# Summing z on VectorE instead of TensorE, with the mask from selects, E built later, six residual buffers and one dm step emptied bank by bank

## The chip, the cores and the metric

The kernel runs on one core of one Trainium2 chip. The metric is the device time of one execution in microseconds (us), and the median of several executions is quoted. A profiled execution lists a span, which is some 2 us shorter than the time of the same execution (819.0 us and 820.84 us for the kernel before).

## The reference

The kernel computes the output and all six gradients of a pre-norm linear-attention block that is followed by a SwiGLU feed-forward network (FFN). S is 2048, D is 640, there are 32 heads of 20 columns, and the FFN is 1728 wide. What matters here is the attention forward and one product of the backward pass that is used as filler.

```python
qkv = layernorm(x) @ wqkv                      # q, k, v: 32 heads of 20
phi = lambda t: where(t > 0, t + 1, exp(t)) + 1e-6
pq, pk = phi(q), phi(k)
kv  = einsum("bhsd,bhse->bhde", pk, v)
z   = einsum("bhsd->bhd", pk)                  # the sum over the 2048 tokens
num = einsum("bhqd,bhde->bhqe", pq, kv)
den = einsum("bhqd,bhd->bhq", pq, z)[..., None] + 1e-6
h   = x + (num / den -> [S, D]) @ wo           # the residual tiles xr are rows of x
out = h + FFN(layernorm(h))                    # and then the gradients of all of it
```

## The kernel before

After the first phase (layer norm, q, k and their phi) come some 93 us that the change touches. TensorE computes Y = xnᵀ·pk (five `ps_y` steps), then the heads' blocks of kv (`ps_kvt`), then W2 (`ps_w2t`, which folds kv and wo together), and last the attention output `ps_a` for 16 row tiles. Steps of an independent product, dm = dout·w_downᵀ (`ps_dm`), are put between them. VectorE divides q by its denominator (`normalise`), and SyncE's transposing loads bring the result into the form that `ps_a` needs (`pqsT`). All matmul results go to one pool of four tiles in PSUM, the memory to which every product here is written. Each tile is `[P, 2, 512]` in fp32, and its two halves are called banks. TensorE reuses a tile when another engine has emptied it: in the trace of this kernel `ps_dm` at 137.19 starts 0.04 us after the end of ScalarE's copy (from 136.34, 0.81 us) for which it waits.

```python
psum = ctx.enter_context(tc.tile_pool(name="psum", bufs=4, space=bass.MemoryType.PSUM))
work = ctx.enter_context(tc.tile_pool(name="work", bufs=5))       # xr, zs, zl and others
# ... the sum z, on TensorE: four groups of tokens, each in 32 rows
        ps = mm("ps_z")
        for ci, (n0, n1) in enumerate(NCH):
            for t in range(ST):
                q = t % 4 * H
                nc.tensor.matmul(ps[q:q + H, ci, :320], lhsT=ones[:, :H], rhs=pk[:, t, n0:n1],
                                 start=(t < 4), stop=(t >= ST - 4))
        zs = [wk("zs"), wk("zl")]                                  # high and low part in bf16
        nc.scalar.copy(out=half(zs[0][:]), in_=row(ps))
        last_zs = nc.vector.tensor_tensor(out=half(zs[1][:]), in0=row(ps), in1=half(zs[0][:]), op=ALU.subtract).ins
# ... a dm step: ten products, one copy by ScalarE
                ps = mm("ps_dm")
                dm_mm(ps, wdT3 if g == 3 else wdT, t, g)
                nc.scalar.copy(out=dst[:, :, :w], in_=ps[:, :, :w])
                if g == 3:
                    nc.scalar.dma_start(out=scr_dm_v[:, t:t + 2, :], in_=dst[:, :, :w])
# ... masks(): E by selects, then mask = Eᵀ E by two matmuls (cut)
# ... normalise(t): q*z, sum per head, + 1e-6, reciprocal, multiply; four row tiles at once (cut)
        for i in range(DT):
            ps = mm("ps_y")
            mm_row(ps, lambda t: xn[:, t, i * P:(i + 1) * P], lambda t, n0, n1: pk[:, t, n0:n1], ST)
            nc.scalar.copy(out=half(Yt[:, i, :]), in_=row(ps))
            if i == 0:
                mm_row(ps_z, lambda k: ones32[:], lambda k, n0, n1: zs[k][:, n0:n1], 2)   # "ps_zb"
                nc.scalar.copy(out=half(zb[:]), in_=row(ps_z))
                masks()
            if 0 < i < 4:
                dm(1)
        dm(1)
        for t in (0, 4):
            normalise(t)
            tr_pqs(t)                      # four transposing loads on SyncE
        for t in range(3):
            load_xr(t)                     # residual tile, on SyncE
        nc.sync.dma_start(out=mat_v(scr_Yt), in_=Yt)
        # ... ps_kvt; dm(1); five ps_w2t with W2's transposes on SyncE, one dm(1) among them
        for t in (8, 12):
            normalise(t)
            tr_pqs(t)
        dm(3)
        for t in range(ST + 2):            # "the loop"
            if t < ST:
                xr = xrs.pop(t)
                ps = mm("ps_a")
                mm_row(ps, lambda i: pqsT[:, i, t * P:(t + 1) * P], lambda i, n0, n1: W2[:, i, n0:n1], DT)
                nc.vector.tensor_tensor(out=half(xr[:]), in0=row(ps), in1=half(xr[:]), op=ALU.add)
                # ... statistics of xr
                dm(1)
            if t > 0:
                load_xr(t + 2)
            u = t - 2
            # ...
            nc.scalar.dma_start(out=scr_h1_v[:, u, :], in_=h1[:])      # h1 is xr of tile u
            # ... hn (VectorE), hnT (a transposing load on SyncE)
```

Note for later what stands in ScalarE's instruction queue in the loop. It issues the stores of `h1` and of the last `dm` group, and between these stores stand its copies that empty the `ps_dm` buffers.

## Time and profile before

| | kernel before |
|---|---|
| time, median of 3 (range) | 821.44 us (821.32 to 822.36) |
| span of the profiled execution, clock | 819.0 us, 1.000 |
| TensorE busy | 812.0 us |
| VectorE / ScalarE / GpSimd busy | 442.4 / 291.0 / 188.2 us |
| first `ps_z` to first `pg` of the FFN, "the stretch" | 55.72 to 149.12 = 93.40 us |
| from the first `pg` to the end | 669.90 us |

The page and TensorE's timeline are read in the prediction below.

### The profile page before, as it was taken

How to read it: one execution, taken by the hardware profiler on the slowest of the kernel's cores; microseconds unless marked ns; L12 is line 12 of the kernel's file. 1: busy time of each engine (PE TensorE's matmuls, PEld its weight loads, DVE VectorE, ACT ScalarE, POOL GpSimd, SP SyncE). 2: the span in 40 equal slices, each digit the busy share in tenths (PEclk: the TensorE clock that was granted, in tenths of full speed). 3: DMA queues.
4: the chain of work that ended last, by engine and by line, in shares of the span. 5: the costliest groups of instructions: out<-in, count | busy, mean ns of one | idle time of the engine just before them, and what ended most of it. 6: DMA issues, size and time to landing. Idle time of an engine off the chain costs nothing.

```text
span 819.0 us, 14057 instructions
## 1 busy us (share of the span) xinstructions
PE 812.0 (99%) x5540; PEld 521.7 (64%) x5540; DVE 442.4 (54%) x874; ACT 291.0 (36%) x412; POOL 188.2 (23%) x345
## 2 busy tenths in 40 slices
PE   8999999999999999999999999999999999999998
PEld 6776656555555555555566677777777777777675
DVE  6878676891077018810660147787793366631212
ACT  6982422770084126500741122322322133322010
POOL 3330022322412312221125301211220111112330
PEclk9999999999999999999999999999999999999999
DMA  9994589999759997894498757977498999999962
GB/s 301 195 356 86 140 175 280 244 226 214 198 123 206 208 207 178 183 249 115 98 233 185 258 123 217 219 206 181 110 224 178 172 174 165 176 204 259 227 177 75
DMA packets 278321, 158.61 MB, mean 194 GB/s; under 512 B 235052, under 2 KB 264877, under 8 KB 278256
## 3 DMA queue, kind: packets, MB, share of 16 engines
q1 hardware_dynamic: 251696, 82.12, 53.1%
q0 software_dynamic: 17744, 64.45, 26.6%
q10 hardware_dynamic: 8816, 11.16, 4.3%
q8 instruction: 43, 0.70, 0.4%
q14 instruction: 22, 0.18, 0.1%
HBM read 47.68 MB, written 53.66 MB: 124 GB/s over the span
## 4 chain that ended last, share of the span: by engine, by line
PE 92%; DVE 4%; ACT 2%; DMA 1%; issue 1%; POOL 0%; DVEq 0%; ACTq 0%
PE ps_dw L627 21%; PE ps_dhn L109 14%; PE ps_dxn L871 8%; PE ps_o L932 7%; PE pu L563 7%; PE pg L558 7%; PE ps_dwqk L109 5%; PE ps_dm L385 5%; PE ps_y L109 3%; PE ps_dp L109 3%; PE ps_dk L109 3%; PE ps_gt L678 3%; PE ps_a L109 3%; PE pdm L385 2%; DVE st L134 1%; ACT phi_e L307 1%
## 5 line engine op out<-in xcount | busy, mean ns | idle before, releaser
L109 PE MATMUL ps_dhn<-wgT,cols 128*128 128x320 bf16 x864 | 119.5, 299 | 0.0
L627 PE MATMUL ps_dw<-dd,hn 128*128 128x448 bf16 (+1 forms) x640 | 118.8, 346 | 0.0
L109 PEld LDWEIGHTS <-cols 128*128 128x128 bf16 x864 | 84.5, 98 | 32.9
L627 PEld LDWEIGHTS <-hn 128*128 128x128 bf16 x640 | 62.6, 98 | 54.2
L629 DVE CAST dwev<-ps_dw 128x896 bf16<-128x896 f32 (+3 forms) x12 | 10.9, 908 | 123.5 <-PE ps_dw L627 123.5
L629 ACT CAST dwev<-ps_dw 128x896 bf16<-128x896 f32 (+1 forms) x20 | 17.6, 878 | 157.9 <-PE ps_dw L627 146.7
L592 POOL DMA_DIRECT2D scr_dT<-stg x64 | 34.8, 543 | 168.7 <-DMA stg<-dd 163.2
L147 DVE CUSTOM_DVE_ANT_0 lb_a<-lb_dy,hn 128x640 bf16<-128x640 bf16 x32 | 26.4, 826 | 75.3 <-ACT lb_dy L145 75.3
L558 PE MATMUL pg<-wgu,hnT 128*128 128x448 bf16 (+1 forms) x320 | 63.6, 346 | 0.0
L563 PE MATMUL pu<-wgu,hnT 128*128 128x448 bf16 (+1 forms) x320 | 63.6, 346 | 0.0
L932 PE MATMUL ps_o<-wd,mT 128*128 128x320 bf16 (+3 forms) x462 | 61.3, 295 | 0.0
L627 PE MATMUL ps_dw<-m_s,dh 128*128 128x448 bf16 (+1 forms) x320 | 60.4, 346 | 0.0
L871 PEld LDWEIGHTS <-ring 128*128 128x128 bf16 x480 | 47.0, 98 | 18.2
L932 PEld LDWEIGHTS <-mT 128*128 128x128 bf16 (+1 forms) x462 | 41.8, 97 | 17.6 <-issue 2.6
L871 PE MATMUL ps_dxn<-wqkvT,ring 128*128 128x320 bf16 x320 | 51.3, 299 | 0.0
L563 PEld LDWEIGHTS <-hnT 128*128 128x128 bf16 x320 | 31.3, 98 | 27.1
L627 PEld LDWEIGHTS <-dh 128*128 128x128 bf16 x320 | 31.3, 98 | 27.1
L558 PEld LDWEIGHTS <-hnT 128*128 128x128 bf16 x320 | 31.3, 98 | 27.0
L298 PE MATMUL ps_kq<-wqk,xnT 128*128 128x320 bf16 x320 | 46.4, 299 | 1.4 <-ACT xnT L290 1.4
L385 PEld LDWEIGHTS <-dh2T 128*128 128x128 bf16 x320 | 31.1, 98 | 25.8 <-issue 0.9
L385 PE MATMUL ps_dm<-wdT,dh2T 128*128 128x448 bf16 (+1 forms) x240 | 46.8, 344 | 0.6 <-ACT dmst L399 0.5
L145 ACT ACTIVATE lb_dy<-ps_dhn,rstd 128x640 bf16<-128x640 f32 x16 | 12.7, 793 | 87.8 <-PE ps_dhn L109 87.8
(162 smaller groups left out, 1277.8 us busy)
## 6 DMA issues: line engine op xcount, KB each, us to landing
scr_dT<-stg POOLq DMA_DIRECT2D x48, 224.0 KB, 3.0
cols<-scr_dT POOLq DMA_DIRECT2D x6, 1728.0 KB, 8.1
scr_m<-m_s POOLq DMA_DIRECT2D x12, 448.0 KB, 4.4
cols<-scr_dT ACTq DMA_DIRECT2D x2, 1728.0 KB, 9.5
out_dram<-dwev POOLq DMA_DIRECT2D x30, 112.0 KB, 3.3
scr_dT<-stg POOLq DMA_DIRECT2D x16, 192.0 KB, 2.6
scr_pk<-pk SPq DMA_DIRECT2D x4, 640.0 KB, 7.5
scr_pq<-pqa SPq DMA_DIRECT2D x4, 640.0 KB, 7.8
```

The costliest lines, as they stand in the source:

```text
L109: nc.tensor.matmul(ps[:, ci, :320], lhsT=lhs(k), rhs=rhs(k, *NCH[ci]), start=(start and k == 0), stop=(stop and k == n - 1))
L147: nc.vector.tensor_tensor_reduce(out=a[:], in0=dy[:], in1=xhat, scale=1.0, scalar=0.0, op0=ALU.mult, op1=ALU.add, accum_out=sums[:, 1:2])
L298: nc.tensor.matmul(ps[:, ci, :320], lhsT=xnT[:, t, k, :], rhs=wqk[:, k, w0 + n0:w0 + n1], start=(k == 0), stop=(k == DT - 1))
L385: nc.tensor.matmul(ps[:, c, :w], lhsT=dh2T[:, kt, (t + c) * P:(t + c + 1) * P], rhs=wdT[:, kt, o:o + w], start=(kt == 0), stop=(kt == DT - 1))
L558: nc.tensor.matmul(pg[:, c, :w], lhsT=hnT[:, kt, (t + c) * P:(t + c + 1) * P], rhs=wg[:, kt, 0:w], start=(kt == 0), stop=(kt == DT - 1))
L563: nc.tensor.matmul(pu[:, c, :w], lhsT=hnT[:, kt, (t + c) * P:(t + c + 1) * P], rhs=wg[:, kt, w:2 * w], start=(kt == 0), stop=(kt == DT - 1))
L592: nc.gpsimd.dma_start(out=scr_dT[t + c, :, KO[g]:KO[g] + GK[g], :], in_=stg[:, :GK[g], :])
L627: nc.tensor.matmul(ps[:, c, :w], lhsT=lhs(t), rhs=rhs(t), start=(t == 0), stop=(t == ST - 1))
L629: copy(out=ev[:, :len(parts), :w], in_=ps[:, :len(parts), :w])
L678: nc.tensor.matmul(ps[:, ci, :320], lhsT=dh1[:, t, i * P:(i + 1) * P], rhs=pqs_tm[:, t, n0:n1], start=(t == 0), stop=(t == ST - 1))
L871: nc.tensor.matmul(ps[:, ci, :320], lhsT=lhs[:, i, :], rhs=rhs[:, i, n0:n1], start=(k == 0 and i == 0), stop=(k == 2 and i == DT - 1))
L932: nc.tensor.matmul(po(t, ci), lhsT=mTs[t // 4][r, t % 4, j, :], rhs=wd[r, j, n0:n1], start=(t, ci) not in opened, stop=last)
```

## The change

The intent is to take z and the mask from TensorE, which is busy 99% of the span, and to take some waits from the loop:

- VectorE sums z from `pk` in fp32, by seven adds of two row tiles at once and one of the halves. TensorE then only broadcasts it (`ps_zb`), in the middle of the third `ps_y`.
- The mask is made by GpSimd's selects at the beginning, and E, which is needed only late, behind the FFN.
- `normalise` is split in two, and the multiply of the second block goes behind `ps_kvt`.
- Six residual tiles are loaded in front, into six buffers.
- One `ps_dm` step (t = 8 of the first group) is emptied by two copies, one bank each, written into the queue after each five products.

```diff
-    work = ctx.enter_context(tc.tile_pool(name="work", bufs=5))
+    work = ctx.enter_context(tc.tile_pool(name="work", bufs=6))
 # ... mask by memset and two pairs of affine_select on GpSimd at the beginning; masks() removed
-        ps = mm("ps_z")
-        # ... its 32 matmuls, the copy and the subtraction
+        with tc.issue_after(last_phi):
+            nc.vector.tensor_tensor(out=z2, in0=tok2[:, 0], in1=tok2[:, 1], op=ALU.add)      # 1280 columns, fp32
+        for t in range(2, ST // 2):
+            nc.vector.tensor_tensor(out=z2, in0=z2, in1=tok2[:, t], op=ALU.add)
+        nc.vector.tensor_tensor(out=zf, in0=zf, in1=z2[:, D:], op=ALU.add)
+        zs = [wk("zs"), wk("zl")]
+        nc.vector.tensor_copy(out=zs[0][:], in_=zf)
+        nc.vector.tensor_tensor(out=zs[1][:], in0=zf, in1=zs[0][:], op=ALU.subtract)
 # ... in the five ps_y steps:
+                if (i, ci) == (2, 0):
+                    z_bcast()
 # ... dm_steps:
+                if g == 0 and t == 8:
+                    dm_mm(ps, wdT, t, g, lambda c: nc.scalar.copy(out=dst[:, c, :w], in_=ps[:, c, :w]))
+                else:
                     dm_mm(ps, wdT3 if g == 3 else wdT, t, g)
                     nc.scalar.copy(out=dst[:, :, :w], in_=ps[:, :, :w])
 # ... the order of the normalise steps:
-        for t in (0, 4):
-            normalise(t)
-            tr_pqs(t)
-        for t in range(3):
+        norm_den(0)
+        norm_mul(0)
+        tr_pqs(0)
+        norm_den(4)
+        for t in range(6):
             load_xr(t)
         nc.sync.dma_start(out=mat_v(scr_Yt), in_=Yt)
         kv_blocks(KVT, "ps_kvt", ...)
+        norm_mul(4)
 # ... W2 and its transposes
-        for t in (8, 12):
-            normalise(t)
-            tr_pqs(t)
+        tr_pqs(4)
+        norm_den(8)
+        norm_mul(8)
+        tr_pqs(8)
+        # ... the same for 12
 # ... the loop:
-            if t > 0:
-                load_xr(t + 2)
+            if t > 2:
+                load_xr(t + 3)
 # ... E: memset, two selects and three loads on GpSimd, after the last gradient product of the FFN
```

More of the change, by code (lines that the diff above doesn't have):

```diff
@@ L233 @@
         nc.vector.memset(ones[:], 1.0)
-        E = const.tile([P, D], BF16, name="E")
-    ones32 = const.tile([P, P], BF16, name="ones32")
-    nc.vector.memset(ones32[:], 1.0 / H)
+        mask = const.tile([P, 160], BF16, name="mask")
+        nc.gpsimd.memset(mask[:], 1.0)
+        for c0, n, p0 in ((0, 6, 0), (120, 2, 88)):
+            m = mask[:, c0:c0 + n * Dh]
+            for sign in (1, -1):
+                nc.gpsimd.affine_select(
+                    out=m, in_=m, pattern=[[-sign * Dh, n], [0, Dh]], compare_op=ALU.is_ge, fill=0.0,
+                    base=-p0 if sign > 0 else p0 + Dh - 1, channel_multiplier=sign)
     zpad = const.tile([P, 4, 64], BF16, name="zpad")
     nc.vector.memset(zpad[:], 0.0)
-    mask = const.tile([P, 160], BF16, name="mask")
+    E = const.tile([P, D], BF16, name="E")
     zb = const.tile([P, D], BF16, name="zb")
@@ L318, in kq_phi @@
                                     op0=ALU.min, op1=ALU.add)
-            nc.vector.tensor_tensor(out=half(dst[:, t, :]), in0=e[:, :, :320], in1=r[:, :, :320], op=ALU.add)
+            last = nc.vector.tensor_tensor(out=half(dst[:, t, :]), in0=e[:, :, :320], in1=r[:, :, :320], op=ALU.add)
         if last and t % 4 == 3:
@@ L324, in kq_phi @@
             nc.sync.dma_start(out=scr_xnT[sl].rearrange("t p k c -> p t k c"), in_=xnT[:, sl])
+        return last.ins
     with tc.manual_schedule(engines={EngineType.PE, EngineType.DVE, EngineType.Activation}):
@@ L362, with dm_mm @@
                 ln1_xn(t - ST + NC)
-        kq_phi(ST - 1)
-        ps = mm("ps_z")
-        for ci, (n0, n1) in enumerate(NCH):
-            for t in range(ST):
-                q = t % 4 * H
-                nc.tensor.matmul(ps[q:q + H, ci, :320], lhsT=ones[:, :H], rhs=pk[:, t, n0:n1],
-                                 start=(t < 4), stop=(t >= ST - 4))
-        zs = [wk("zs"), wk("zl")]
-        nc.scalar.copy(out=half(zs[0][:]), in_=row(ps))
-        last_zs = nc.vector.tensor_tensor(out=half(zs[1][:]), in0=row(ps), in1=half(zs[0][:]), op=ALU.subtract).ins
-        ps_z = mm("ps_zb")
+        last_phi = kq_phi(ST - 1)
     dm_t = {0: strips.tile([P, ST, GM], BF16, name="dm0", tag="S")}
-    def dm_mm(ps, wdT, t, g):
+    def dm_mm(ps, wdT, t, g, each=None):
         w = GW[g]
@@ L386, in dm_mm @@
                                  rhs=wdT[:, kt, o:o + w], start=(kt == 0), stop=(kt == DT - 1))
+            if each:
+                each(c)
     def dm_steps():
@@ L396, in dm_steps @@
                 ps = mm("ps_dm")
-                dm_mm(ps, wdT3 if g == 3 else wdT, t, g)
                 dst = dmst[:, t // 2] if g == 3 else dm_t[g][:, t:t + 2, :]
-                nc.scalar.copy(out=dst[:, :, :w], in_=ps[:, :, :w])
+                if g == 0 and t == 8:
+                    dm_mm(ps, wdT, t, g, lambda c: nc.scalar.copy(out=dst[:, c, :w], in_=ps[:, c, :w]))
+                else:
+                    dm_mm(ps, wdT3 if g == 3 else wdT, t, g)
+                    nc.scalar.copy(out=dst[:, :, :w], in_=ps[:, :, :w])
                 if g == 3:
@@ L408, in dm @@
             next(dms, None)
-    def masks():
-        tc.keep_in_program_order(nc.gpsimd.memset(E[:H, :], 1.0))
-        for sign in (1, -1):
-            tc.keep_in_program_order(nc.gpsimd.affine_select(
-                out=E[:H, :], in_=E[:H, :], pattern=[[sign, D]], compare_op=ALU.is_ge, fill=0.0,
-                base=0 if sign > 0 else Dh - 1, channel_multiplier=-sign * Dh))
-        for q in range(H, P, H):
-            nc.gpsimd.dma_start(out=E[q:q + H, :], in_=E[:H, :])
-        ps = mm("ps_mask")
-        pm = ps[:, 0, :160]
-        nc.tensor.matmul(pm[:, :120], lhsT=E[:H, 0:P], rhs=E[:H, 0:120], start=True, stop=True)
-        nc.tensor.matmul(pm[:, 120:], lhsT=E[:H, D - P:D], rhs=E[:H, 600:D], start=True, stop=True)
-        nc.scalar.copy(out=mask[:], in_=pm)
     pqsT = big.tile([P, DT, S], BF16, name="pqsT", tag="B")
@@ L432, in hb4, with norm_den @@
         return ap.rearrange("p t (h e) -> p t h e", e=Dh)
-    def normalise(t):
+    def norm_den(t):
         pq = pqa[:, t:t + 4, :]
@@ L442, in normalise, with norm_mul @@
         nc.vector.reciprocal(out=rall[:, t:t + 4, :], in_=den[:])
+    def norm_mul(t):
+        pq = pqa[:, t:t + 4, :]
         nc.vector.tensor_tensor(out=hb4(pq), in0=hb4(pq), in1=bc4(rall[:, t:t + 4, :]), op=ALU.mult)
@@ L459, with z_bcast @@
         KVT = yk[:, DT * D:].rearrange("p (j c) -> p j c", j=HG)
-        with tc.issue_after(last_zs):
-            nc.vector.memset(KVT, 0.0)
+        z2 = tzs[:, 4:8].rearrange("p t d -> p (t d)").bitcast(FP32)
+        zf = z2[:, :D]
+        tok2 = pk.rearrange("p (t two) d -> p t (two d)", two=2)
+        with tc.issue_after(last_phi):
[6 more added lines that the diff above has]
+        nc.vector.tensor_tensor(out=zs[1][:], in0=zf, in1=zs[0][:], op=ALU.subtract)
+        nc.vector.memset(KVT, 0.0)
+        def z_bcast():
+            ps = mm("ps_zb")
+            mm_row(ps, lambda k: ones[:], lambda k, n0, n1: zs[k][:, n0:n1], 2)
+            nc.scalar.copy(out=half(zb[:]), in_=row(ps))
         for i in range(DT):
             ps = mm("ps_y")
-            mm_row(ps, lambda t: xn[:, t, i * P:(i + 1) * P], lambda t, n0, n1: pk[:, t, n0:n1], ST)
+            for ci, (n0, n1) in enumerate(NCH):
+                for t in range(ST):
+                    nc.tensor.matmul(ps[:, ci, :320], lhsT=xn[:, t, i * P:(i + 1) * P], rhs=pk[:, t, n0:n1],
+                                     start=(t == 0), stop=(t == ST - 1))
+                if (i, ci) == (2, 0):
+                    z_bcast()
             nc.scalar.copy(out=half(Yt[:, i, :]), in_=row(ps))
-            if i == 0:
-                mm_row(ps_z, lambda k: ones32[:], lambda k, n0, n1: zs[k][:, n0:n1], 2)
-                nc.scalar.copy(out=half(zb[:]), in_=row(ps_z))
-                masks()
             if 0 < i < 4:
@@ L499 @@
             nc.sync.dma_start_transpose(out=W2[:, :, i * P:(i + 1) * P], in_=W2T[:, i, :])
-        for t in (8, 12):
-            normalise(t)
-            tr_pqs(t)
+        tr_pqs(4)
+        norm_den(8)
+        norm_mul(8)
+        tr_pqs(8)
+        norm_den(12)
+        norm_mul(12)
+        tr_pqs(12)
         dm(3)
@@ L628, in dw @@
                 ev = fw("dwev")
-                copy(out=ev[:, :len(parts), :w], in_=ps[:, :len(parts), :w])
+                last = copy(out=ev[:, :len(parts), :w], in_=ps[:, :len(parts), :w])
                 for c, (_, _, dst) in enumerate(parts):
                     nc.gpsimd.dma_start(out=dst[:, GO[g]:GO[g] + w], in_=ev[:, c, :w])
+                return last
             def dwd_part(i):
@@ L645 @@
                         load_cols(1, act_load)
-                dw([dgu_part(i, 0), dgu_part(i, 1)], nc.scalar.copy)
+                last_dw = dw([dgu_part(i, 0), dgu_part(i, 1)], nc.scalar.copy)
     wB.close()
+    wait_for(last_dw, [nc.gpsimd.memset(E[:H, :], 1.0)])
+    for sign in (1, -1):
+        nc.gpsimd.affine_select(
+            out=E[:H, :], in_=E[:H, :], pattern=[[sign, D]], compare_op=ALU.is_ge, fill=0.0,
+            base=0 if sign > 0 else Dh - 1, channel_multiplier=-sign * Dh)
+    for q in range(H, P, H):
+        nc.gpsimd.dma_start(out=E[q:q + H, :], in_=E[:H, :])
     M = ctx.enter_context(tc.tile_pool(name="M", bufs=1))
```

## The prediction

> **What bounds the kernel now.** I read the page first: busy shares, then the granted clock.
>
> ```profile
> PE 812.0 (99%) x5540; PEld 521.7 (64%) x5540; DVE 442.4 (54%) x874; ACT 291.0 (36%) x412; POOL 188.2 (23%) x345
> ...
> PEclk9999999999999999999999999999999999999999
> ```
>
> TensorE works for 812.0 of 819.0 us at full clock, in every slice. A change can therefore win only what it takes from TensorE's own stream, plus what it takes from some 7 us of idle time, most of which lies in the first microseconds. Second, the view of waits, for TensorE alone:
>
> ```profile
> PE ps_warm L332 <- POOL ident masks.py:199: 1.4, 1, 1.4
> PE ps_kq L298 <- ACT xnT L290: 1.4, 2, 1.1
> PE ps_dm L385 <- ACT dmst L399: 0.5, 1, 0.5
> PE ps_t L284 <- DVE xn L278: 0.3, 1, 0.3
> PE ps_z L370 <- DVE pk L319: 0.2, 1, 0.2
> ```
>
> The change touches only the last of these and the 0.5 us before ps_dm. So the timeline decides, between the end of the first phase and the start of the FFN (55 to 149 us). The columns are start, duration, engine, line, operation, and the wait before it.
>
> ```profile
> 55.72 0.72 PE L370 MATMUL ps_z<-pk,ones 128*32 128x320 bf16 x15
> 57.26 0.49 DVE L319 TENSOR_TENSOR pqa<-phi_e,phi_r 128x640 bf16<-128x640 bf16 x1 [0.27 <-ACT phi_r L308]
> 57.38 4.52 PE L109 MATMUL ps_y<-pk,xn 128*128 128x320 bf16 x32
> ...
> 62.14 0.30 PE L109 MATMUL ps_zb<-zl,ones 128*128 128x320 bf16 x1
> ...
> 62.55 4.19 PEld L109 LDWEIGHTS <-xn 128*128 128x128 bf16 x32
> ...
> 63.26 1.49 DVE L438 TENSOR_TENSOR tzs<-pqa,zb 128x2560 bf16<-128x2560 bf16 x1 [3.81 <-ACT zb L468]
> ...
> 87.97 1.54 DVE L486 TENSOR_TENSOR yk<-ps_kvt,mask 128x120 bf16<-128x120 f32 x6 [7.90 <-PE ps_kvt L484]
> ...
> 106.17 0.82 DVE L513 TENSOR_TENSOR xr<-ps_a,xr 128x640 bf16<-128x640 f32 x1
> ...
> 108.13 2.05 PE L385 MATMUL ps_dm<-wdT,dh2T 128*128 128x448 bf16 x10
> ```
>
> The reader is to see three things. The sum z costs TensorE 57.38 - 55.72 = 1.66 us. VectorE has two long rests (3.81 and 7.90 us). And VectorE comes to the first residual tile (106.17) only after the four normalise steps, while TensorE is already two row tiles further. The PSUM pool has four tiles of two banks, so TensorE runs ahead of VectorE by that much only. The semaphores of the trace show that the ps_dm step at 108.13 waits for VectorE: it reuses the buffer that the add of 106.17 empties at 106.99. The slack is 1.1 us.
>
> [...]from operations with an fp32 operand: 128x640 read from PSUM takes 825 ns[...], and the 128x2560 multiply with the fp32 reciprocals takes 2825 ns[...]. No run yet has the copy. [...]This trace has a 1.3 us pause at 13.95 with clock 1.000 throughout, so I expect a pause of 2 us to cost only itself.
>
> **The change, part by part.**
> (1) *z leaves TensorE.* ps_y starts where ps_z started: -1.66 us. Its sixteenth token is not a new wait: it comes at 55.72 + 15 x 0.136 = 57.8, and its pk is written at 56.55.
> (2) *The mask product goes.* The last zb product starts at 62.14 and the next ps_y at 62.55; a spacing of 0.14 is normal, so -0.27 us. The selects at the beginning are five short GpSimd instructions (0.2 to 0.3 us each) behind the identity, done before GpSimd is asked for the first rstd at 4.85: 0.
> (3) *z on VectorE.* It begins when pqa is done, about 57.70. Seven adds of 1280 fp32: [...]about 0.035 between dependent ones (63.26 to 64.78 for a 1.49 us operation): 10.7. One add of 640: 0.86. [...]The remainder zl: 0.83. Sum 12.9, so zl is there at about 70.6.
> TensorE gets to the zb products in the middle of the third ps_y: 55.75 + 2 x 4.36 (ps_y, from 62.55 to the ps_dm at 66.91) + 1.89 (one ps_dm) + 2.18 (half a ps_y) = 68.54. The zl product would start at 68.68 and can start at 70.65: **a new wait of about +2.0 us**. So ps_kvt starts at 87.6, where it was 87.5: what (1) and (2) win is gone there.
> (4) *VectorE arrives later at the residual.* The last zb product ends near 71.2, ScalarE's copy at 72.0; the first normalise starts at 72.04, not 63.26. Full step of the first block and the denominators of the second: 5.62 + 2.75 + 5.62 = 14.0, at 86.0, so the mask multiplies of ps_kvt are still on time (88.1 to 89.55). But the multiply of the second block (2.75) now lies behind them, and then come the same 16.73 us as before (89.44 to 106.17): the first residual add starts at 109.0 and ends at 109.85. The ps_dm step that was at 108.13 would be there at about 108.0: **+1.9 us** if it gets the same buffer. Buffers are given out by the scheduler: with a luckier choice 0.3, with the ps_a step in front of it waiting instead, 3.2. ScalarE's queue makes it no better: its copy of the ps_dm before (107.39) stands behind a store of the same residual tile. I take +1.6, and +0.3 for catching up: VectorE needs 2.3 us a row tile against TensorE's 3.25, thus three or four tiles for 3 us.
> (5) *Six residual buffers.* VectorE waits 7.8 us for these loads in all. TensorE feels it twice: a start interval of 0.37 in place of 0.19 at 116.71, and the chain below:
>
> ```profile
> 132.32 1.37 PE ps_a L109 x10
> 133.69 0.83 DVE xr L513
> ...
> 136.34 0.81 ACT dmst L399
> 137.19 1.78 PE ps_dm L385 x10
> ```
>
> There ps_dm starts 0.83 after the last ps_a instead of 0.14. Together -0.87 us. A load is then issued one row tile (3.25 us) earlier relative to its use, and it lands in 3.2 us, so I expect nearly all of it back.
> (6) *One ps_dm emptied bank by bank.* The next ps_dm starts 92.10, 0.29 after the last ps_w2t product, where 0.05 is normal: about -0.2 us.
> (7) *E behind the FFN.* Memset and selects of 0.6, 0.7, 0.7 us and three issues on GpSimd, near 463 us, where GpSimd then waits 6.98 us before its next load. Needed at 620: 0.
> Sum: -1.66 - 0.27 + 2.0 + 1.9 - 0.87 - 0.2 = **+0.9 us**. I shade it to +0.8, as the change looks tuned (the split of the normalise step keeps ps_kvt on time).
>
> **Rivals.**
> *A plain gain.* If z were ready on arrival at 68.5, and VectorE made up its delay in its rests, the change would win 1.66 + 0.27 + 0.87 + 0.2 = 3.0 us: 818.4. For it: VectorE rests 11.7 us in these 50 us. Against: the fp32 work of 12.9 us is longer than the 10.9 us between 57.7 and 68.6, and the remaining rest lies before ps_kvt, with the dependent work behind it.
> *One of the two waits only.* The zb wait but no buffer wait: 821.4 + 0.9 - 1.9 = 820.4. This hangs on the scheduler.
> *VectorE as the bound into the loop.* The wait moves to the earlier ps_a, and ScalarE's copies, queued behind stores of residual tiles, hold further buffers: +2.5 to +3.5 us, 824 to 825.
> *The transfers were hidden anyway.* Then (5) brings only the 0.2 us of 116.71: 0.7 us worse than the sum.
>
> **Range and chances.** Centre 821.44 + 0.8 = 822.2. Low end: buffer wait absent and the z chain half a microsecond quicker, 819.8. High end: late buffers, no gain from the loads, 824.6. Repeats lie within 1 us (821.32 to 822.36). Two per cent is 16.4 us; no term here is over 3.3. Faster by over 2%: 0.005; within 2%: 0.985; slower: 0.01.
>
> **What the changed profile should show.** ps_y begins at 55.7 with no ps_z before it. VectorE has seven fp32 adds of about 1.5 us from 57.7. TensorE waits some 2 us at the zb product, with zl as its releaser. The first ps_kvt starts within 0.3 of 87.6. The first residual add is near 109.0, and a TensorE wait of 1 to 3 us for VectorE lies between 106 and 111. The residual loads appear no more as VectorE's releaser, and the 0.5 us before ps_dm at 137 is gone. From the FFN on both traces run alike, shifted by the difference. It would be wrong [...]if the clock dropped in the 2 us pause, or if the scheduler dealt the buffers otherwise.

The time of an add in (3) can be estimated from the two operations with an fp32 operand that the trace of the kernel before shows: 0.825 us for 640 columns and 2.825 us for 2560, so 0.825 + 640 x 2.000 / 1920 = 1.49 us for 1280. Seven of these with their gaps of 0.035 us are the 10.7 us. The sum of 12.9 us also holds 0.52 us for the copy of z to bf16 and its gap; that was the estimate, which no trace had shown.

## More of the kernel before

One more view matters for the result: the timeline of SyncE's queue. Its columns are start, time taken, engine and line, operation, and count. This one is of the kernel before.

```profile
99.75 12.86 SPq L447 DMA_TRANSPOSE pqsT<-pqa  x8
112.66 1.07 SPq L454 DMA_DIRECT2D xr<-in_A_x_dram  x2
...
119.42 0.56 SPq L454 DMA_DIRECT2D xr<-in_A_x_dram  x1
```

SyncE issues one thing after the other here. After the five transposes of W2 come the last eight of pqsT, whose issue ends at 112.61. Only after those, from 112.66, come the residual tiles that follow the three loaded in front. The load at 119.42 is that of tile 6, counted from 0.

## The result, and the profile after

| | before | after |
|---|---|---|
| time, median of 4 each (range) | 821.38 us (821.25 to 822.36) | 823.65 us (823.09 to 825.35) |
| ratio after / before, 95% interval | | 1.0028 (1.0011 to 1.0046) |
| span of the profiled execution, clock | 819.0 us, 1.000 | 821.7 us, 1.000 |
| TensorE / VectorE busy | 812.0 / 442.4 us | 811.0 / 453.9 us |
| the stretch to the first `pg` | 93.40 us | 55.94 to 151.87 = 95.93 us |
| first `pg` to the end | 669.90 us | 669.86 us |

A ratio is the mean time of one kernel's runs over that of the other's of the same rounds, so it is not quite the ratio of the medians. Within 2% the two are the same; the changed kernel is about a quarter of a per cent slower. The difference of the two spans is 2.7 us. Of that, 2.5 us lie in the stretch and 0.2 us in when it begins.

The first line of the page of the changed kernel gives busy time, share of the span and instructions of each engine:

```profile
PE 811.0 (99%) x5506; PEld 520.6 (63%) x5506; DVE 453.9 (55%) x882; ACT 290.4 (35%) x411; POOL 188.9 (23%) x350
```

And this is its view of waits for TensorE: engine and tile, line, releaser, then us in total, times and the longest.

```profile
PE ps_dm L379 <- ACT dmst L398: 1.3, 3, 0.5
PE ps_zb L109 <- DVE zs L456: 1.2, 1, 1.2
PE ps_dm L379 <- ACT dm L395: 0.6, 1, 0.6
...
PE ps_zb L109 <- DVE zl L457: 0.5, 1, 0.5
...
PE ps_dm L379 <- ACT dm L398: 0.4, 1, 0.4
PE ps_a L109 <- DMA wvo<-wvo: 0.2, 1, 0.2
```

TensorE works less, but it waits more: the broadcast of z for VectorE (two entries), the bank-wise step and later `ps_dm` steps for ScalarE (three), and the first `ps_a` for a load. Of these the kernel before had only 0.5 us of the dmst entry. The timeline of the changed kernel shows the chain of z. The bracket gives the idle time before an instruction and what ended it.

```profile
57.98 1.48 DVE L451 TENSOR_TENSOR tzs<-pk 128x1280 f32<-128x1280 bf16 x1
...
59.50 9.13 DVE L453 TENSOR_TENSOR tzs<-tzs,pk 128x1280 f32<-128x1280 f32 x6
...
69.52 0.49 DVE L456 CAST zs<-tzs 128x640 bf16<-128x640 f32 x1
...
70.07 0.31 PE L109 MATMUL ps_zb<-zs,ones 128*128 128x320 bf16 x1 [1.18 <-DVE zs L456]
...
70.93 0.30 PE L109 MATMUL ps_zb<-zl,ones 128*128 128x320 bf16 x1 [0.55 <-DVE zl L457]
...
72.26 1.49 DVE L422 TENSOR_TENSOR tzs<-pqa,zb 128x2560 bf16<-128x2560 bf16 x1 [0.98 <-ACT zb L463]
```

Seven adds of about 1.5 us and their tail last from 57.98 to 70.9, and TensorE is there first. VectorE then starts the first normalise step at 72.26, where the kernel before had it at 63.26. The next lines are the bank-wise step:

```profile
89.42 1.11 PE L379 MATMUL ps_dm<-wdT,dh2T 128*128 128x448 bf16 x5
...
90.56 0.53 ACT L395 CAST dm<-ps_dm 128x448 bf16<-128x448 f32 x1 [1.58 <-PE ps_dm L379]
...
91.14 1.10 PE L379 MATMUL ps_dm<-wdT,dh2T 128*128 128x448 bf16 x5 [0.62 <-ACT dm L395]
```

The five products of the second bank do not overlap the copy of the first. They start at 91.14, 0.05 us after it ends (90.56 and 0.53 us), although the two touch different banks, and what they wait for is a semaphore of ScalarE: in this trace the dependency holds for the whole tile (e2 tests this). And this is SyncE's queue and the loop of the changed kernel:

```profile
93.44 7.56 SPq L505 DMA_TRANSPOSE wvo<-wvo  x5
101.10 17.19 SPq L434 DMA_TRANSPOSE pqsT<-pqa  x12
...
109.26 0.82 DVE L523 TENSOR_TENSOR xr<-ps_a,xr 128x640 bf16<-128x640 f32 x1
...
109.36 2.06 PE L379 MATMUL ps_dm<-wdT,dh2T 128*128 128x448 bf16 x10
...
121.69 0.59 SPq L441 DMA_DIRECT2D xr<-in_A_x_dram  x1
...
124.85 0.33 ACTq L539 DMA_DIRECT2D scr_h<-xr  x1
125.23 0.91 ACT L398 CAST dm<-ps_dm 128x896 bf16<-128x896 f32 x1 [3.00 <-DMA xr<-in_A_x_dram]
...
126.18 1.78 PE L379 MATMUL ps_dm<-wdT,dh2T 128*128 128x384 bf16 x10 [0.41 <-ACT dm L398]
```

As `normalise` is late, twelve transposes of pqsT and not eight stand behind those of W2. They hold SyncE until 118.29, where they held it until 112.61 before. So the load of tile 6 is issued at 121.69, later than with five buffers (119.42). And ScalarE's copy at 125.23, which reads nothing but PSUM, is released by that load: in its queue stands a store (124.85) that waited for it, though it stores another tile; the load landed at 124.78. `ps_dm` at 126.18 waits for the copy. The copy's own products had started at 119.11 and were done at 121.2, so it began 4.1 us late. A late copy does no harm by itself, only when TensorE needs the tile: here the copy at 121.33 began 3.4 us late and `ps_dm` at 122.36 did not wait, and in e4, below, one began 3.4 us late and the loop had no wait.

To add this up I counted for each wait the interval between two starts of matmuls, less what is normal for the pair; this is a little more than the bracket shows. Without waits the stretch is the same number in every kernel with the same work, which checks the count:

| us | before | after |
|---|---|---|
| the broadcast of z | 0 | 2.07 |
| the step at 91 to 92 | 0.25 | 0.79 |
| first `ps_a`, for W2's transposes | 0 | 0.37 |
| the loop | 0.89 | 2.41 |
| sum of waits | 1.14 | 5.64 |
| stretch less waits | 92.26 | 90.29 |

The work fell by 1.97 us and the waits rose by 4.50 us; that is the 2.5 us.

### The profile page after: what moved, and what is told of

It reads as the page before. It is cut to its first block, busy times and chain, and to the rows that moved or that the text cites. A ratio compares the mean times of both kernels' runs of the same rounds, so it can differ in the third digit from the quotient of the medians.

```text
span 821.7 us, 13986 instructions
## 1 busy us (share of the span) xinstructions
PE 811.0 (99%) x5506; PEld 520.6 (63%) x5506; DVE 453.9 (55%) x882; ACT 290.4 (35%) x411; POOL 188.9 (23%) x350
## 4 chain that ended last, share of the span: by engine, by line
PE 86%; DVE 8%; DMA 2%; ACT 2%; issue 1%; POOL 0%; DVEq 0%; ACTq 0%; SPq 0%
PE ps_dw L637 21%; PE ps_dhn L109 14%; PE ps_dxn L889 8%; PE ps_o L950 7%; PE pg L568 7%; PE pu L573 7%; PE ps_dwqk L109 5%; PE ps_dk L109 3%; PE ps_gt L696 3%; PE ps_dp L109 3%; PE ps_dm L379 2%; DVE st L134 2%; PE pdm L379 2%; PE ps_y L469 1%; DVE tzs L453 1%
## 5 line engine op out<-in xcount | busy, mean ns | idle before, releaser
L147 DVE CUSTOM_DVE_ANT_0 lb_a<-lb_dy,hn 128x640 bf16<-128x640 bf16 x32 | 26.4, 826 | 74.6 <-ACT lb_dy L145 70.9
```

Of the source, the lines that this page charges most:

```text
L147: nc.vector.tensor_tensor_reduce(out=a[:], in0=dy[:], in1=xhat, scale=1.0, scalar=0.0, op0=ALU.mult, op1=ALU.add, accum_out=sums[:, 1:2])
```

## The experiments

All kernels gave right results. The time of the kernel before in these rounds was a median of 821.2 to 821.8 us. The waits are counted as above, in the one profiled execution of each run, and a dash means none of 0.19 us or more. In the kernels with z on TensorE the 1.66 us of `ps_z` are in the rest.

| run | time, median (range), us | ratio to before (95%) | stretch | z | step at 91 | W2 | loop | rest |
|---|---|---|---|---|---|---|---|---|
| e1 | 823.7 (823.37 to 824.6) | 1.0024 (1.0008 to 1.004) | 95.46 | 2.07 | 0.25 | 0.98 | 1.82 | 90.3 |
| e2 | 823.19 (822.46 to 824.17) | 1.0018 (1.0001 to 1.0036) | 94.51 | 2.07 | 0.31 | 0.61 | 1.18 | 90.3 |
| e3 | 822.58 (821.97 to 822.98) | 1.0008 (0.9992 to 1.0024) | 94.86 | - | 0.79 | 0.93 | 2.84 | 90.3 |
| e4 | 823.04 (822.22 to 823.55) | 1.0014 (0.9998 to 1.003) | 95.21 | 2.07 | 0.79 | 1.98 | - | 90.4 |
| e5 | 821.23 (820.82 to 822.46) | 0.9993 (0.9975 to 1.0011) | 92.95 | - | 0.79 | 0.19 | - | 92.0 |
| e6 | 820.8 (820.29 to 823.77) | 0.9992 (0.9971 to 1.0013) | 93.30 | - | 0.25 | - | 0.67 | 92.4 |
| e8 | 824.09 (823.88 to 825.54) | 1.0031 (1.0014 to 1.0047) | 95.99 | - | 0.31 | - | 3.46 | 92.2 |
| e9 | 821.7 (820.53 to 823.2) | 0.9999 (0.9981 to 1.0017) | 92.54 | - | 0.31 | - | - | 92.2 |
| e10 | 822.68 (821.71 to 823.62) | 1.0009 (0.9991 to 1.0027) | 95.02 | 2.06 | 0.79 | 0.37 | 1.49 | 90.3 |
| e11 | 820.96 (819.97 to 823.31) | 0.999 (0.9972 to 1.0009) | 92.35 | - | 0.31 | 0.21 | 1.49 | 90.3 |
| e12 | 823.69 (823.38 to 824.82) | 1.0024 (1.0008 to 1.004) | 95.58 | 2.06 | 0.79 | 0.76 | 1.67 | 90.3 |
| e13 | 818.82 (818.44 to 820.33) | 0.9963 (0.9935 to 0.9991) | 90.85 | - | 0.31 | - | - | 90.5 |

The theory was that the late z makes every later transfer late: SyncE's queue is longer, the residual loads come late, and ScalarE's copies stand behind stores that wait for transfers. The rivals were that each wait has its own cause and its own price (so undoing one part brings back what it costs), and that VectorE's own work is the bound. e12 is the changed kernel once more, as a yardstick.

> The changed kernel again, timed on the same chip and in the same rounds as the two runs beside it: 823.1 to 824.0 if its first measurement of 823.65 holds; its trace should show the same waits at zb (2.1 us), in the split ps_dm (0.8), at the first ps_a for W2 (0.4) and in the loop (about 2.4 in all).

It repeats the time (823.69 us). It also shows how much a single wait moves between executions: W2 0.76 in place of 0.37, and the loop 1.67 in place of 2.41. The two together are 2.43 and 2.78. So differences of some tenths in one column are not read below.

### e1 and e2: the bank-wise step

e1 is the changed kernel with the bank-wise step undone.

```diff
-                if g == 0 and t == 8:
-                    dm_mm(ps, wdT, t, g, lambda c: nc.scalar.copy(out=dst[:, c, :w], in_=ps[:, c, :w]))
-                else:
-                    dm_mm(ps, wdT3 if g == 3 else wdT, t, g)
-                    nc.scalar.copy(out=dst[:, :, :w], in_=ps[:, :, :w])
+                dm_mm(ps, wdT3 if g == 3 else wdT, t, g)
+                nc.scalar.copy(out=dst[:, :, :w], in_=ps[:, :, :w])
```

> The changed kernel with the one ps_dm step copied out in one piece again, all else as changed. My theory: the 0.79 us that TensorE loses inside that step (its second bank waits for ScalarE's copy of the first, although the two share no bank) goes, and the old 0.25 us before the next ps_dm comes back: 0.5 us faster than the changed kernel, 823.1. Rival: the weights W2 come through the transposing loads at their own time (TensorE waits 0.37 us for them at 102.18), so what is won at 91 is lost at 102 and the time stays at 823.6.

The 0.79 us went and the 0.25 us of the kernel before came back, so the split has a net cost of 0.54 us where it stands. The time didn't move (823.7 us). In the profiled execution the first `ps_a` waited longer for W2's transposes (0.98), as the rival said. That the saving always goes there is not shown: in e12 this wait was 0.76 us with no edit at all.

e2 keeps two copies, but writes both after all ten products.

```diff
+                dm_mm(ps, wdT3 if g == 3 else wdT, t, g)
                 if g == 0 and t == 8:
-                    dm_mm(ps, wdT, t, g, lambda c: nc.scalar.copy(out=dst[:, c, :w], in_=ps[:, c, :w]))
+                    for c in range(2):
+                        nc.scalar.copy(out=dst[:, c, :w], in_=ps[:, c, :w])
                 else:
-                    dm_mm(ps, wdT3 if g == 3 else wdT, t, g)
                     nc.scalar.copy(out=dst[:, :, :w], in_=ps[:, :, :w])
```

> The changed kernel, still with two copies, one a bank, but both written in the program after all ten matmuls of the step. My theory: what costs is only the program order (a matmul that stands behind a copy from the same PSUM tile waits for it), so the 0.79 us goes, and the first copy still starts before the second bank is full, so that the old 0.25 us does not come back: 0.8 us faster than the changed kernel, 822.8. Rival: the split itself costs (two copies of 0.53 us in place of one of 0.91) and the time stays within 0.2 us of 823.6, or the first copy waits for the whole tile and it equals the run with one copy, 823.1.

The 0.79 us went here too, and 0.31 us stayed before the next step. So two copies by themselves give no gain over one, and it was the copy between the products that made TensorE wait. The time fell by some 0.5 us, less than the runs of one kernel differ.

### e3: the broadcast of z half a step later

```diff
-                if (i, ci) == (2, 0):
+                if (i, ci) == (2, 1):
                     z_bcast()
```

> The changed kernel with the zb products after the whole third ps_y block (half a block, 2.2 us, later). Theory A: TensorE's wait of 2.07 us for zs and zl is a plain loss, VectorE starts the normalise steps at nearly the same time, and 1.8 us are won: 821.8. Theory B (mine): VectorE then sets the pace further down: the first residual add still ends near 110.1, TensorE is 1.8 us earlier at the ps_a tile that waits for it (111.26, slack 1.2 us) and at the residual loads, and only 0.3 to 1.2 us are won: 822.4 to 823.3.

The wait of 2.07 us is gone. The stretch is 1.07 us shorter and the time 1.1 us lower; the rest went into W2 and the loop. VectorE lost nothing by it: its first residual add came at 107.41, 1.85 us earlier, as the work that follows waits for `ps_kvt` anyway, which TensorE reached earlier. So the wait for z was a real loss, but only half of the whole.

### e4: twelve residual tiles loaded in front

Tiles 6 to 11 are put into buffers that the first phase has left.

```diff
-            xrs[t] = wk("xr")
+            xrs[t] = wk("xr") if t not in range(6, 12) else wpool.tile([P, D], BF16, name="xr_f", tag="f", bufs=6)
 ...
-        for t in range(6):
+        for t in range(12):
             load_xr(t)
 ...
             if t > 2:
-                load_xr(t + 3)
+                load_xr(t + 9)
```

> The changed kernel with twelve residual tiles loaded in front (the further six in buffers of the first phase, which are free then), so that no residual load up to tile 11 stands in SyncE's queue behind the twelve transposing loads of pqsT. My theory: these late loads (issued 121.69 and after, the add of tile 6 waits until 124.86) cause the four waits of ps_dm for ScalarE at 126, 133, 136 and 140, 2.4 us together, and at least 1.5 us are won: 822.1 or less. Rival: ScalarE's queue order (copies behind the stores of h1, which follow VectorE) causes them, so that VectorE's waits for loads go but the ps_dm waits stay, and the time stays within 0.5 us of 823.6.

All waits of the loop went, so late residual loads were at their root, at least in part: TensorE also came to the second half of the first `ps_a` 1.6 us later after the start of the stretch, which alone gives later transfers more time. The time fell by some 0.6 us, less than the 1.5 us expected. The wait for W2's transposes rose to 1.98 us, as these timeline lines of e4 show:

```profile
89.23 2.77 SPq L441 DMA_DIRECT2D xr_f<-in_A_x_dram  x6
92.10 0.40 SPq L483 DMA_DIRECT2D scr_Yt<-yk  x1
93.62 8.91 SPq L505 DMA_TRANSPOSE wvo<-wvo  x5
...
103.97 0.85 PE L109 MATMUL ps_a<-wvo,pqsT 128*128 128x320 bf16 x5 [1.62 <-DMA wvo<-wvo]
```

Six more loads stand in front of the store of Y (92.10, where the changed kernel had it at 89.04). The five transposes of W2 then take 8.91 us to issue instead of 7.56, and the first of them lands 6.5 us after its issue instead of 4.3. So the loads need more than buffers: they need a place where they don't delay a more urgent transfer.

### e5 and e6: z back on TensorE, and the buffers alone

e5 is the changed kernel with z and the order of `normalise` as before; mask, E, six buffers and the bank-wise step stay.

```diff
-        with tc.issue_after(last_phi):
-            nc.vector.tensor_tensor(out=z2, in0=tok2[:, 0], in1=tok2[:, 1], op=ALU.add)
-        # ... the other adds, the copy, the subtraction
+        ps = mm("ps_z")
+        # ... its 32 matmuls, the copy and the subtraction, as before
 ...
         norm_den(4)
+        norm_mul(4)
+        tr_pqs(4)
```

> The changed kernel with z summed by TensorE again, and the normalise steps in their old order; mask, E, the six buffers and the split ps_dm stay as changed. My theory: the fp32 chain on VectorE is behind both the 2.07 us wait at zb and most of the 2.4 us in the loop (late normalise, late transposing loads, late residual loads). So both go, 1.66 and 0.3 us of ps_z come back, the 0.79 us in the split step stays: 821.0 to 821.7, some 2.3 us faster than the changed kernel. Rival: the loop's waits come from the six buffers or from ScalarE's queue whatever VectorE does: then only the 2.07 us are swapped for 2.0 us and the time stays at 823.5.

The time is 821.23 us: this part of the change, z with the order of `normalise` that goes with it, carries its loss. No wait in the loop is left. The balance to the kernel before closes: -0.27 (mask) + 0.54 (step) + 0.19 (W2) - 0.89 (loop) = -0.43, and the stretch is 0.45 us shorter. Against the changed kernel, z on VectorE is worth -1.66 + 2.07 + 0.18 + 2.41 = +3.0 us, and the stretch differs by 2.98.

e6 is the kernel before with six buffers alone.

```diff
-    work = ctx.enter_context(tc.tile_pool(name="work", bufs=5))
+    work = ctx.enter_context(tc.tile_pool(name="work", bufs=6))
 ...
-        for t in range(3):
+        for t in range(6):
             load_xr(t)
 ...
-            if t > 0:
-                load_xr(t + 2)
+            if t > 2:
+                load_xr(t + 3)
```

> The kernel before with the six residual buffers alone. My theory: with VectorE in time the loads are early enough, the 0.19 and 0.70 us that TensorE loses at 116.71 and 137.19 go, and perhaps 0.3 us come back at the first ps_a, because three more loads and a later store of Y compete with the loads of W2: 820.5 to 821.0, 0.4 to 0.9 us faster than before. Rival: the six buffers by themselves do harm (a later W2 and the same waits): 821.4 to 822.5.

Here each load of tile 6 and later is issued some 3 us earlier than before (tile 6 at 116.69 instead of 119.42, tile 9 at 124.87 instead of 127.83). Still the wait near 137 stays, with 0.67 us of the 0.70. TensorE waits there for ScalarE, whose copy stood behind a store until 136.63. The semaphores of the trace (counters by which engines and transfers tell that they are done; each transfer makes 16 updates in the traces of the kernel before and of the changed kernel) show for what that store (136.27) waited: the load of FFN weights that SyncE had issued at 128.34 and that landed at 136.20. In the kernel before it is the same load (issued 128.45, landed 135.90, store at 135.98). So the buffers give less than 0.3 us alone, and the prediction had put that wait down to the wrong transfer. The time (820.8 us) can't be told from that of the kernel before.

### e8 and e9: the mended order

e8 takes e3 and e2 together, puts the store of Y behind W2's transposes, and loads tiles 6 to 11 there.

```diff
-                if (i, ci) == (2, 0):
+                if (i, ci) == (2, 1):
 ...
-        nc.sync.dma_start(out=mat_v(scr_Yt), in_=Yt)
         # ... ps_kvt, W2 and its transposes
+        nc.sync.dma_start(out=mat_v(scr_Yt), in_=Yt)
+        for t in range(6, 12):
+            load_xr(t)
         tr_pqs(4)
```

> The changed kernel with its four new waits mended: zb after the whole third ps_y block, the two copies of the split ps_dm behind all of its matmuls, the store of Y behind the loads of W2, and six more residual tiles loaded there. My theory: waits of 2.07 (zb), 0.5 (split step), 0.4 (W2) and 2.4 us (loop) go: 818.3 to 819.3, which beats the kernel before by 2 to 3 us. Rival: VectorE, 3 us later than before, then holds TensorE at the PSUM tiles of the first residual adds, and the gain stops at 820.5 to 821.5.

This was a miss: 824.09 us, slower than the changed kernel. The first half was as expected: the first `ps_a` came 42.68 us after the start of the stretch, where the changed kernel had 45.19. Then two `ps_dm` waited for ScalarE, and from 123.00 to 127.60, where the second ended (123.22), the granted clock was 0.63. These are timeline lines of e8, and below them one line of the table by stretches (from and to, length, busy us and instructions of PE, PEld, DVE, ACT and POOL, clock, DMA share, GB/s):

```profile
113.27 2.06 PE L379 MATMUL ps_dm<-wdT,dh2T 128*128 128x448 bf16 x10
...
116.78 5.45 ACTq L542 DMA_DIRECT2D scr_h<-xr  x2
...
122.27 0.91 ACT L399 CAST dm<-ps_dm 128x896 bf16<-128x896 f32 x1 [4.68 <-DVE xr_f L526]
...
123.22 3.11 PE L379 MATMUL ps_dm<-wdT,dh2T 128*128 128x448 bf16 x10 [2.18 <-ACT dm L399]
```

```profile
123.00:127.60 4.60, 4.38 (x16) 2.06 (x16) 0.39 (x2) 1.08 (x2) 0.87 (x2) 0.63 0.93 248
```

The products that the copy at 122.27 empties had started at 113.27 and taken 2.06 us, so they were done at 115.3, and the copy began 6.9 us late; two stores stood in ScalarE's queue in front of it. The semaphores of the trace show for what the second of them (121.90) waited: the completion of a transfer that SyncE had issued at 119.33, the store of KVT, which landed at 121.82 and with which it has no data in common. The trace of the changed kernel has the same pair: the store of KVT, issued at 118.34 on semaphore 106, lands at 120.82, and ScalarE, which waits for that semaphore, issues a store of `h1` on it at 120.92. In the traces of the kernel before and of the changed kernel, all transfers issued by SyncE and by ScalarE use eight completion semaphores (100 and 102 to 108), and those issued by GpSimd eight others (111 to 118). Of the 639 transfers of each, 623 follow another one on the same semaphore, and every one of these was issued after that one had landed, the closest by 0.02 us. This suggested that the queue, and not the data, was the cause. The slow clock cost another 1.7 us, an estimate from 4.60 us at 0.63. It came with two pauses of TensorE within 6 us, of 0.95 and 2.18 us, while in the changed kernel a wait of 2.07 us, broken by one product, left the clock at 1.00 (69 to 72); whether it takes both pauses or the longer one alone is not shown. But two of the six executions had a mean clock of 1.000 and took 823.88 and 824.06 us, so e8 is as slow without the slow clock; where these two lost their time no trace shows.

e9 is the same mended order with z on TensorE.

> The same mended kernel, but with z on TensorE as before. My theory: TensorE's stream has the 1.66 us of ps_z and its 0.33 us wait again, so 820.2 to 820.8, which is 1.5 to 2 us slower than with z on VectorE. Rival: z on VectorE costs as much elsewhere, and the two are within 0.5 us of one another.

It came out at 821.7 us, the same as before. Its profiled execution shows no wait in the loop, but one of 1.8 us at 694.9 that no other run here has, and its times spread over 2.7 us. So no gain of the mended order with z on TensorE is shown, and none is ruled out.

### e10 and e11: the stores of h1 issued by GpSimd

The same line is changed in the changed kernel (e10) and in e8 (e11).

```diff
-            nc.scalar.dma_start(out=scr_h1_v[:, u, :], in_=h1[:])
+            nc.gpsimd.dma_start(out=scr_h1_v[:, u, :], in_=h1[:])
```

> The changed kernel with the sixteen stores of h1 issued by GpSimd instead of ScalarE; everything else as changed. My theory: ScalarE's copies of ps_dm are ready long before, but stand behind stores of h1 that wait for a DMA completion semaphore which the late loads and stores of SyncE use too; TensorE waits for these copies. Without the stores in ScalarE's queue the four waits of ps_dm (2.4 us together) go, though VectorE and the residual loads are as late as before: 821.0 to 821.8, some 2.2 us faster than the changed kernel. Rival: VectorE's lateness itself holds the PSUM tiles (the ps_a tiles that its adds empty), so that ps_a or ps_dm wait for VectorE instead and less than 0.8 us is won: 822.9 to 823.6.

> The mended kernel with z on VectorE (late zb, copies of the split step behind its matmuls, store of Y behind the loads of W2, twelve residual tiles in front) and the stores of h1 on GpSimd. My theory: it had 1.9 us less than the kernel before when it came to the first ps_a, and lost 5 us only to ScalarE's queue and to the clock drop behind the long wait; so with free copies it ends at 818.5 to 819.5, 2 to 3 us faster than the kernel before. Rival: VectorE, whose first residual add comes at 107.3, then holds PSUM and the gain stops at 820.5 or more.

From e8 to e11 the time fell by 3.1 us (824.09 to 820.96) with the order of all data unchanged. The waits at 117 and 123 and the slow clock are gone from the trace. The queue was the cause. Still e11 missed its 818.5 to 819.5, and from the changed kernel to e10 the time fell by 1.0 us where 2.2 were expected. VectorE still waited 9.5 us for residual loads in e10, but TensorE felt only 1.49 us in the loop, 0.51 of them from VectorE's own late add: a late load hurts mostly through the copies that stand behind it. The timeline of e10 shows for what the copies still waited:

```profile
136.21 0.80 ACT L398 CAST dmst<-ps_dm 128x768 bf16<-128x768 f32 x1 [4.21 <-DMA wgu<-in_B_w_gate_dram]
...
140.86 0.80 ACT L398 CAST dmst<-ps_dm 128x768 bf16<-128x768 f32 x1 [3.85 <-DMA wgu<-in_B_w_up_dram]
```

Two copies out of PSUM are released by loads of FFN weights, which they do not read. Here the other stores of ScalarE's queue do it, those of `dm`.

### e13: all stores of the loop issued by GpSimd

```diff
                 if g == 3:
-                    nc.scalar.dma_start(out=scr_dm_v[:, t:t + 2, :], in_=dst[:, :, :w])
+                    nc.gpsimd.dma_start(out=scr_dm_v[:, t:t + 2, :], in_=dst[:, :, :w])
```

> The version e11 (z on VectorE late, both copies of the split step after its ten products, store of Y and the middle residual loads behind the W2 transposes, residual stores issued by GpSimd) with the stores of the last dm group issued by GpSimd too. Theory: the two waits that e11 still had near the end of the loop (0.93 us at 138.89 and 0.56 at 142.42, ps_dm released by ScalarE's copies, which stand behind a store that waits for a weight load's DMA) go, as ScalarE then issues no DMA there: stretch from the first ps_y to the first pg about 90.9 to 91.2 us instead of 92.35, time 819.3 to 819.9, faster than the kernel before by 1.3 to 2 us. Rival A: the wait for the shared DMA semaphore moves to GpSimd, whose reciprocal root of the next tile then comes late by 4 us; the normalised tile and its transpose come late, and the first FFN products wait for them: stretch 92 to 93, time as e11. Rival B: the waits were from VectorE's side (residual loads of the last tiles), then they stay where they are: stretch 92.3.

The time is 818.82 us against 821.19 us, and the interval of the ratio (0.9935 to 0.9991) leaves out 1, though it overlaps that of e11, which ran on another chip. One of the eleven runs of the kernel before took 828.07 us at a lower clock (0.995) and counts; without it the ratio of the means is 819.02 / 821.14 = 0.9974. This version beats both kernels, the kernel before by some 0.3%. The kernel before with the same stores on GpSimd was not run, so how much of this is due to z on VectorE is not shown by times; the traces without waits in the loop give 1.7 us for it (e13's stretch of 90.85 against e9's 92.54). These are the largest wait of TensorE after the first phase, from e13's view of waits, and one of the copies in the loop, from its timeline:

```profile
PE pg L571 <- DMA hnT<-hn: 1.4, 1, 1.4
```

```profile
136.99 0.80 ACT L399 CAST dmst<-ps_dm 128x768 bf16<-128x768 f32 x1 [2.18 <-PE ps_dm L379]
```

Each copy of the loop now waits only for its products, and no wait of TensorE in the loop is over 0.2 us. The rival that the delay comes back in the FFN is right in part: in the profiled execution `pg` waited 1.4 us, at 172.4, for the last transposed tiles hnT. Their issue ran from 152.21 to 171.48, when large loads had begun. GpSimd's reciprocal root was not the cause: the last one was done at 151.1. That execution was the slowest of the six (820.33 us), so the others may not have this wait; no trace shows it.

One thing could not be tried. Moving the transposes of pqsT into the loop, so that they don't hold SyncE's queue, ended in a deadlock.

## Why the prediction was right or wrong

The time was in the range (822.2 predicted, 823.65 measured), and the sign of the small difference was right. The terms of the sum fared as follows.

- **(1) and (2), work that leaves TensorE: right.** -1.66 and -0.27 us predicted; the stretch without waits fell by 1.97. `ps_y` begins at 55.94 with nothing before it.
- **(3), the fp32 chain and the new wait: right.** +2.0 us predicted, 2.07 measured. `zl` was to be ready at 70.6 and the product that needs it started at 70.93. The adds took 1.48 to 1.49 us (1.49 by the estimate from the trace before), 1.52 apart. The copy took 0.49 us; what the sum held for it had been shown by no run. `ps_kvt` came at 87.87 (87.6), and the clock stayed at 1.000.
- **(4), "The ps_dm step that was at 108.13 would be there at about 108.0: +1.9 us if it gets the same buffer": this step failed.** The first residual add came at 109.26, where 109.0 was predicted, so VectorE was as late as worked out. But no wait lies between 106 and 111. The `ps_dm` at 109.36 got another buffer, which its predecessor's copy by ScalarE had emptied: the semaphore that it waits for is ScalarE's, where that of the `ps_dm` at 108.13 before was VectorE's. The prediction had named this chance and not taken it.
- **(5), "I expect nearly all of it back": wrong in sign.** -0.87 us predicted; the loop's waits rose from 0.89 to 2.41. The step overlooked SyncE's queue. A buffer that is free early is no use here, as the load stands behind twelve transposes (17.19 us of issue), and these are late because z is. e5 shows the loop free of waits with z early. e6 shows that the wait at 137 wasn't the residual load's at all: it stayed with six buffers, and its store waited for a load of FFN weights. e13, without stores in ScalarE's queue, is free of it.
- **(6), the bank-wise step: wrong in sign.** -0.2 us predicted, +0.54 measured (0.25 before, 0.79 after; e1). The products of the second bank wait for the copy of the first.
- **(7) E and the selects: right in cost.** Nothing after the first `pg` changed (669.90 and 669.86 us). But the four selects were not done before the first rstd: they ran at 8.51 and from 10.39 to 11.3, between GpSimd's other work. The stretch began 0.2 us later than before, which is within what its start varies over the runs (55.7 to 57.5).
- **Not foreseen:** the first `ps_a` waits 0.37 us for W2's transposes, behind three more loads.

So the +1.9 us of (4) never came, and (5), (6) and the unforeseen term brought instead 1.52 + 0.54 + 0.37 = 2.43, where (5) and (6) were to bring -1.07. The errors, -1.9 and +3.5 us, cancelled in part, and +1.6 was left: +0.9 was the sum and +2.5 the outcome. That the time stayed in the range is luck in this sense, as two of the terms had the wrong sign and one was absent. Of the rivals, "VectorE as the bound into the loop" comes nearest. It named ScalarE's copies behind the stores, which e10, e11 and e13 show to be the path; VectorE's arithmetic was not the bound, since e11 and e13 keep all of it.

What is shown: the z chain's wait (e3), the cost of the split (e1, e2), that late loads stand behind the loop's waits (e5, and e4 in part), and that they reach TensorE by way of the stores in ScalarE's queue (e8 to e11, e13). What is inferred from the semaphore numbers of traces alone is that the stores wait because completion semaphores are shared. What stays open is the 1.4 us at hnT in e13, the single wait of e9, what the executions of e8 at full clock waited for, and what the kernel before would gain from the stores on GpSimd alone.

## What to carry to other kernels

Work moved off the busiest engine is worth only what the waits leave of it: follow the result of the moved work through every queue that it makes late, above all the transfers that stand behind it. Don't let an engine that empties PSUM issue DMAs in a loop that is bound by TensorE; here in the changed kernel the copies began up to 4.6 us after their products were done, behind stores that waited for transfers which neither of them touches, and taking the stores away turned a kernel that lost 2.3 us into one that, with the broadcast half a step later and the loads in a better order, wins 2.4 us. Count what the stretch would take without waits: a number that is equal in all variants with the same work (here 90.3 to 90.5 us with z on VectorE and full clock) says that no large wait has been missed.
